# Two output tiles of a fused attention and MLP kernel leave in column halves on two queues

## The chip, the cores and the metric

The kernel runs on one core of a Trainium2 chip. The metric is the device time of one execution in microseconds (us); lower is better. One core has five engines with an instruction stream each: TensorE (PE, matrix products; its weight loads are shown apart as PEld), VectorE (DVE), ScalarE (ACT), GpSimd (POOL) and SyncE (SP, which here only issues transfers and waits). Engines and transfers signal each other by semaphores. A transfer counts its semaphore up in 16 steps, and has landed with the sixteenth.

## The reference

For each of 8 batches and 8 heads (576 positions, 64 features), Nystroem attention with 32 landmarks, and then an MLP with a squared ReLU over all 4608 rows:

```python
A, Bm, C = sm(q, k_lm), sm(q_lm, k_lm), sm(q_lm, k)   # softmax of scaled products
Z = Bm.T / (norm1(Bm) * norminf(Bm) + 1e-6)
for _ in range(6):
    Z = 2 * Z - Z @ Bm @ Z
x = heads_side_by_side(A @ Z @ C @ v)                 # 4608 x 512
out = (maximum(x @ w_in, 0) ** 2) @ w_out             # 512 -> 2048 -> 512, float32
```

`q_lm` and `k_lm` are means over segments of 18 positions.

## The kernel before, in words

The batches are worked through one after the other. For each, the attention part leaves a factor `AT` (with the rows of A) and a product `G` of the rest with `w_in`, so that the first layer of the MLP is `G` times `AT` (`mlp_in`, L821). ScalarE takes the ReLU out of PSUM (L825), VectorE squares it into `gT` (L826). The second layer (`mlp_out`, L834) runs over pairs of batches, whose 1,152 rows are nine tiles of 128 rows, t = 0 to 8: four from the first batch, one (t = 4) of the two tails of 64 rows, four from the second. Each tile is a sum of 16 products (L852) of 128 x 512 in one PSUM bank. ScalarE copies the bank into an SBUF tile `o_sb` (L863), of which there are three in turn, and the tile leaves for the output in HBM (L832 is the line that the profile gives to these transfers, where `leave` calls them).

The order on PE, DVE, ACT and SP is the order in which the program is written down. Strings of tokens, one for each batch (`PLANS`), say when a first-layer tile, a square, an attention step, or some products of the second layer come. `advance(outs, n)` draws n products from the generator `mlp_out`. So within a batch the second layer fills the gaps of the next batch's attention. At the end, after the last batch's plan, the rest of the second layer is run to its end with nothing beside it (the loop over `outs`).

A tile's transfer is not issued at once. It is put on the list `leaving`, and `leave()` issues what is on it, after the third product of the next tile. In the last batch (`b == B - 1`) `leave()` is called straight after the copy. Transfers of the output go by ScalarE's queue (`nc.scalar.dma_start`), with one exception. The very last tile (`final`: b = 7, t = 8) is computed in two parts, 384 columns and then 128. VectorE copies the first part, which leaves by SyncE's queue (`nc.sync`); ScalarE copies the second, which leaves by its own.

SyncE's queue has also carried one load at the start and the transposing transfers (L283, L284, L588) up to batch 7. After the last of these it holds only that 384-column part.

Every transfer that SyncE or ScalarE issues takes the next of eight queue semaphores, DMAHW0 to DMAHW7, in turn, in the order of the program. Before a semaphore is taken again, its last transfer must have landed. GpSimd's transfers have eight of their own, DMASW0 to DMASW7. At the end of the program (L970) SyncE's queue waits for all of them by nine instructions, each with two conditions: first DMASW7 with DMASW6, then DMAHW0 with DMASW5, DMAHW1 with DMASW4, and so on up to DMAHW6 with VectorE's count and DMAHW7 with ScalarE's count. Then come a drain, and two barriers over all engines. In the kernel before, the two parts of the last tile stand on DMAHW4 (SyncE) and DMAHW5 (ScalarE).

Of the kernel before, what the change touches and what calls it, by code (L numbers as in the profile page):

```python
# [17 lines left out]
B = 8  # L18
# [6 lines left out]
DM = 512  # L25
# [61 lines left out]
def kernel(  # L87
# [9 lines left out]
    nc = tc.nc  # L97
# [166 lines left out]
    def ntile(shape, dt=F32, place=0, placed=True):  # L264
        if not placed:
            place = turn[0] = (turn[0] + 1) % 3
        return psum.tile(shape, dt, tag="n%d" % place, bufs=1, name="n%d" % place)
# [560 lines left out]
    leaving = []  # L828

    def leave():  # L830
        while leaving:
            leaving.pop(0)()  # L832

    def mlp_out(b, gT):  # L834

        b0 = b - b % 2
        for t in range(0, NC4) if b % 2 == 0 else range(NC4, 9):
            first, final = (b, t) == (0, 0), (b, t) == (B - 1, 8)
            if final:
                halves = [psum.tile([P, 2, DM], F32, tag="h", bufs=2, name="ops2")[:, 0, 0:w]  # L840
                          for w in (3 * DM // 4, DM // 4)]
            elif (b // 2 + t) % 2:
                halves = [ntile([P, DM], place=2)[:]]
            else:
                halves = [psum.tile([P, DM], F32, tag="o", bufs=1, name="ops")[:]]
            o_sb = mlp.tile([P, DM], F32, tag="o", bufs=3, name="o_sb")
            lo = 0
            for i, ops in enumerate(halves):
                cols = slice(lo, lo + ops.shape[-1])
                lo = cols.stop  # L850
                for f in range(NF):
                    nc.tensor.matmul(ops, lhsT=gT[:, f, t * P:t * P + P],  # L852
                                     rhs=w_out_bf[:, f, cols],
                                     start=(f == 0), stop=(f == NF - 1))
                    if f == 2:
                        leave()
                    if f < NF - 1:
                        yield
                o_h = o_sb[:, cols]
                if final and i == 0:  # L860
                    nc.vector.tensor_copy(o_h, ops)
                else:
                    nc.scalar.copy(o_h, ops)  # L863
                queue = nc.sync if final and i == 0 else nc.scalar
                if t == NC4:
                    for e in range(2):
                        r0 = (b0 + e) * S + NC4 * P
                        leaving.append(partial(queue.dma_start, out[r0:r0 + TAIL, :],
                                               o_h[64 * e:64 * e + TAIL, :]))
                else:  # L870
                    bb, c = (b0, t) if t < NC4 else (b0 + 1, t - NC4 - 1)
                    rows = out[bb * S:bb * S + NC4 * P, :].rearrange("(p c) n -> p c n", c=NC4)
                    leaving.append(partial(queue.dma_start, rows[:, c, cols], o_h))
                if b == B - 1:
                    leave()
                yield
# [28 lines left out]
    def outputs():  # L905
        for b in range(B):
            yield from mlp_out(b, gTs[b // 2])
# [67 lines left out]
```

## Time and profile before

| | us |
|---|---|
| four times | 259.24, 258.86, 258.98, 257.99; median 258.92 |
| the profiled execution | 259.24 |
| its span, from the first to the last instruction | 257.4 |
| PE busy | 248.0 (96% of the span) |
| ACT busy | 154.3 (60%) |
| DVE busy | 173.4 (67%) |
| last part of PE's work ends | 253.8 |

The profile is one execution of the program. Its times count from the start of the span. The page shows each engine's busy share, the chain of work that ended last, the costliest groups of instructions and the transfers. The chain ends with the last computing instruction: what the queues do after that, from 254.1 to 257.4, stands in the rows of the queues alone. A queue's waits and drains are not counted as busy. A wait is recorded with the moment at which it was satisfied and went through, so the time between two such rows is the time waited. The letter q behind an engine (SPq, ACTq) means its instruction queue.

### The profile page before, as it was taken

How to read it: one execution, taken by the hardware profiler on the slowest of the kernel's cores; microseconds unless marked ns; L12 is line 12 of the kernel's file. 1: busy time of each engine (PE TensorE's matmuls, PEld its weight loads, DVE VectorE, ACT ScalarE, POOL GpSimd, SP SyncE). 2: the span in 40 equal slices, each digit the busy share in tenths (PEclk: the TensorE clock that was granted, in tenths of full speed). 3: DMA queues.
4: the chain of work that ended last, by engine and by line, in shares of the span. 5: the costliest groups of instructions: out<-in, count | busy, mean ns of one | idle time of the engine just before them, and what ended most of it. 6: DMA issues, size and time to landing. Idle time of an engine off the chain costs nothing.

```text
span 257.4 us, 6802 instructions
## 1 busy us (share of the span) xinstructions
PE 248.0 (96%) x2784; PEld 147.1 (57%) x2784; DVE 173.4 (67%) x478; ACT 154.3 (60%) x273; POOL 45.4 (18%) x70
## 2 busy tenths in 40 slices
PE   7688899999999999999999999999999999999994
PEld 2555666565645666466646655566646664566442
DVE  5578989658695788658866887677857778334000
ACT  1566798477654785467735765558727774566210
POOL 8934233100301230150000500610000000000000
PEclk9979999999999999999999999999999999999999
DMA  8999999999999999999849799999468113211122
GB/s 187 197 189 203 206 199 197 193 143 159 170 153 165 132 185 179 205 166 211 142 94 144 155 178 222 169 185 179 115 82 167 43 41 94 81 43 42 41 84 83
DMA packets 81216, 37.48 MB, mean 146 GB/s; under 512 B 48800, under 2 KB 75680, under 8 KB 81184
## 3 DMA queue, kind: packets, MB, share of 16 engines
q0 software_dynamic: 39808, 17.83, 56.4%
q1 hardware_dynamic: 36128, 9.97, 25.1%
q10 hardware_dynamic: 5248, 9.24, 11.9%
q8 instruction: 22, 0.36, 0.6%
q14 instruction: 10, 0.08, 0.1%
HBM read 36.70 MB, written 9.44 MB: 179 GB/s over the span
## 4 chain that ended last, share of the span: by engine, by line
PE 91%; DVE 3%; DMA 3%; POOL 1%; issue 1%; ACT 0%; POOLq 0%
PE ops L852 26%; PE h L821 24%; PE n L852 23%; PE g L804 3%; PE n L527 3%; DMA stage<-in_q_dram 3%; PE n L339 2%; PE n L411 2%; PE n L612 1%; PE n L627 1%; PE n L555 1%; PE n L594 1%; PE idle L292 1%; POOL qkt L132 1%; DVE T L660 1%
## 5 line engine op out<-in xcount | busy, mean ns | idle before, releaser
L825 ACT ACTIVATE r<-h 128x576 bf16<-128x576 f32 x128 | 81.1, 653 | 35.7 <-PE h L821 29.2
L852 PE MATMUL ops<-w_out_bf,gT 128*128 128x512 bf16 (+2 forms) x320 | 82.2, 368 | 0.0
L852 PEld LDWEIGHTS <-gT 128*128 128x128 bf16 x592 | 52.4, 97 | 40.6 <-issue 4.6
L852 PE MATMUL n<-w_out_bf,gT 128*128 128x512 bf16 x272 | 72.8, 379 | 0.0
L821 PE MATMUL h<-AT,G 128*128 128x288 bf16 x448 | 70.6, 286 | 0.0
L826 DVE TENSOR_TENSOR gT<-r 128x576 bf16<-128x576 bf16 x128 | 54.8, 447 | 17.5 <-ACT r L825 16.9
L821 PEld LDWEIGHTS <-G 128*128 128x128 bf16 x512 | 48.0, 98 | 24.1 <-DVE AZ L794 0.6
L701 DVE CAST G<-g 128x1024 bf16<-128x1024 f32 x14 | 17.1, 1223 | 7.9 <-PE g L804 7.6
L701 ACT CAST G<-g 128x1024 bf16<-128x1024 f32 x14 | 14.2, 1013 | 11.7 <-PE g L804 11.6
L132 POOL DMA_DIRECT2D raw<-in_k_dram x5 | 4.4, 889 | 80.1 <-DMA AT<-an 35.8
L863 ACT COPY o_sb<-n 128x512 f32<-128x512 f32 x17 | 10.0, 586 | 14.1 <-PE n L852 12.8
L863 ACT COPY o_sb<-ops 128x512 f32<-128x512 f32 (+1 forms) x19 | 10.8, 570 | 10.4 <-PE ops L852 7.3
L527 PEld LDWEIGHTS <-T 128*128 128x128 bf16 x256 | 11.8, 100 | 4.2 <-issue 0.4
L569 DVE TENSOR_REDUCE ra<-EA 128x20 f32<-128x640 f32 (+3 forms) x19 | 13.3, 703 | 1.1 <-ACT EA L532 1.0
L581 DVE TENSOR_TENSOR an<-EA,rra 128x640 bf16<-128x640 f32 (+2 forms) x18 | 13.1, 738 | 0.1
L527 PE MATMUL n<-bd,T 128*128 128x64 bf16 x256 | 13.1, 197 | 0.0
L532 ACT ACTIVATE EC<-n 128x512 bf16<-128x512 f32 x16 | 9.4, 596 | 3.7 <-PE n L527 3.5
L532 ACT ACTIVATE EA<-n 128x512 f32<-128x512 f32 x16 | 9.6, 599 | 3.3 <-PE n L527 1.9
L416 DVE SCALAR_TENSOR_TENSOR EY<-EY,n 128x128 bf16<-128x128 bf16 x25 | 6.9, 277 | 6.3 <-PE n L411 6.2
L292 PE MATMUL idle<-bd 128*128 128x512 bf16 (+1 forms) x27 | 9.1, 462 | 1.5 <-DVE bd L115 1.5
L821 PE MATMUL h<-AZ,G 128*128 128x288 bf16 x64 | 9.9, 286 | 0.3 <-DVE AZ L794 0.3
L339 PEld LDWEIGHTS <-nat 128*128 128x128 bf16 x256 | 8.3, 96 | 3.1 <-issue 0.6
(144 smaller groups left out, 260.5 us busy)
## 6 DMA issues: line engine op xcount, KB each, us to landing
out_dram<-o_sb ACTq DMA_DIRECT2D x31, 256.0 KB, 4.3
vm<-in_v_dram POOLq DMA_DIRECT2D x8, 512.0 KB, 11.5
raw<-in_k_dram POOLq DMA_DIRECT2D x5, 512.0 KB, 7.1
raw<-in_q_dram POOLq DMA_DIRECT2D x5, 512.0 KB, 8.4
w_in_bf<-in_moe_w_in_dram POOLq DMA_DIRECT2D x4, 512.0 KB, 13.3
w_out_bf<-in_moe_w_out_dram POOLq DMA_DIRECT2D x4, 512.0 KB, 17.2
stage<-in_k_dram SPq DMA_DIRECT2D x1, 1024.0 KB, 5.8
stage<-in_k_dram POOLq DMA_DIRECT2D x2, 512.0 KB, 13.8
```

The costliest lines, as they stand in the source:

```text
L292: nc.tensor.matmul(idle[:, 0:width], lhsT=z[:, 0:P], rhs=z[:, 0:width], start=True, stop=True)
L339: nc.tensor.matmul(means[:, ti, p, :], lhsT=src.rearrange("p h d -> p (h d)"), rhs=seg[:, c + (ti if c == NC4 else 0), :], start=(n == 0 a ...
L527: nc.tensor.matmul(sc[:, c, j, :, :], lhsT=X[nm + "T"][:, c, p, :], rhs=BD[:, 1 if nm == "q" else 0, p, 0:64], start=True, stop=True)
L532: nc.scalar.activation(dst, sc.rearrange("p c j i m -> p c (j i m)"), AF.Exp, scale=SCALE)
L569: nc.vector.reduce_sum(ra[:, quads, lo:hi, :], EA[:, quads, lo:hi, :].rearrange("p q c (h m) -> p q c h m", m=M), axis=AX.X)
L581: on.tensor_tensor(an[:, i, lo:hi, :].rearrange("p c (h m) -> p c h m", m=M), EA[:, i, lo:hi, :].rearrange("p c (h m) -> p c h m", m=M), r ...
L701: (act, dve)[n % 2](G[:, :, n * 512:n * 512 + 512], gg[:])
L821: nc.tensor.matmul(h[:, j, 0:HALF], lhsT=G[:, qd, f * P:(f + 1) * P], rhs=AT[:, qd, a0 + j * HALF:a0 + (j + 1) * HALF], start=(qd == 0), s ...
L825: nc.scalar.activation(r.rearrange("p (j t) -> p j t", j=2), h[:, :, 0:HALF], AF.Relu)
L826: return lambda: nc.vector.tensor_tensor(gT[:, f, o:o + S], r[:], r[:], ALU.mult)
L852: nc.tensor.matmul(ops, lhsT=gT[:, f, t * P:t * P + P], rhs=w_out_bf[:, f, cols], start=(f == 0), stop=(f == NF - 1))
L863: nc.scalar.copy(o_h, ops)
```

## The change

In the last batch the tiles t = 6 and t = 7, the last two whole ones, leave in two halves of 256 columns. The first half goes by the queue that took the whole tile before (ScalarE's), the second by SyncE's. Products, copies and the last tile's two parts stay.

```diff
                     rows = out[bb * S:bb * S + NC4 * P, :].rearrange("(p c) n -> p c n", c=NC4)
-                    leaving.append(partial(queue.dma_start, rows[:, c, cols], o_h))
+                    if b == B - 1 and t in (6, 7):
+                        for side, by in ((slice(0, DM // 2), queue), (slice(DM // 2, DM), nc.sync)):
+                            leaving.append(partial(by.dma_start, rows[:, c, side], o_h[:, side]))
+                    else:
+                        leaving.append(partial(queue.dma_start, rows[:, c, cols], o_h))
                 if b == B - 1:
                     leave()
```

There are two transfers more, both on SyncE's queue, which gets four instructions more: two issues, and ahead of each a wait for its queue semaphore (DMAHW3 and DMAHW5; the issue itself waits for ScalarE's copy). The semaphores of all transfers after them shift: t = 6 takes DMAHW2 and 3, t = 7 takes DMAHW4 and 5, and the two parts of the last tile take DMAHW6 (SyncE) and DMAHW7 (ScalarE). The streams of PE, DVE, ACT and POOL keep their instructions and their order.

## Prediction

> **What bounds the kernel now.** I read the page's chain of waits first, then the chain's last pieces, then the timeline of the last 10 us, and last what the queues do after the last computing instruction.
>
> The page's chain that ended last, and the chain's last pieces in order of time (start, length, what):
>
> ```profile
> PE 91%; DVE 3%; DMA 3%; POOL 1%; issue 1%; ACT 0%; POOLq 0%
> ...
> 246.83 6.96 PE ops L852 x48
> 253.79 0.02 issue
> 253.82 0.27 ACT o_sb L863
> ```
>
> TensorE sets the pace to the end. Its last matmul ends at 253.79, ACT copies the last 128 columns out of PSUM, and at 254.08 computing is over. The span is 257.4, so 3.3 us of it lie behind the last arithmetic. The change touches only output transfers; it can win only there, or lose by coming into that stretch.
>
> The timeline of these microseconds (start, length, engine, line, tile), and the page's row on the output transfers (count, size, us from issue to landing):
>
> ```profile
> 246.87 0.59 ACT L863 COPY o_sb<-n 128x512 f32<-128x512 f32 x1 [2.87 <-PE n L852]
> 247.49 0.34 ACTq L832 DMA_DIRECT2D out_dram<-o_sb  x1
> 250.32 0.59 ACT L863 COPY o_sb<-ops 128x512 f32<-128x512 f32 x1 [2.87 <-PE ops L852]
> 250.94 0.34 ACTq L832 DMA_DIRECT2D out_dram<-o_sb  x1
> 252.98 0.56 DVE L861 COPY o_sb<-ops 128x384 f32<-128x384 f32 x1 [13.60 <-PE ops L852]
> 253.56 0.35 SPq L832 DMA_DIRECT2D out_dram<-o_sb  x1
> ...
> 254.11 0.34 ACTq L832 DMA_DIRECT2D out_dram<-o_sb  x1
> ```
> ```profile
> out_dram<-o_sb ACTq DMA_DIRECT2D x31, 256.0 KB, 4.3
> ```
>
> The rows at 247.49 and 250.94 are t = 6 and t = 7, the two that the change splits; 253.56 and 254.11 are the two pieces of t = 8. The last one decides: it lands 1.8 us after its issue. In the trace's records the sixteenth count of its semaphore is at 255.932; that of SP's piece is at 255.715.
>
> Then SP's queue waits for the queue semaphores at L970, one instruction each, in a fixed order: DMAHW0, 1, ... 7. I asked for line 970 on SP's queue in narrow windows (count, ns min/median/max, first and last start):
>
> ```profile
> L970 SPq EVENT_SEMAPHORE  x5: 28/28/28, 254.0 to 254.2; - x5
> L970 SPq EVENT_SEMAPHORE  x1: 28/28/28, 255.7 to 255.7; - x1
> L970 SPq EVENT_SEMAPHORE  x1: 28/28/28, 255.9 to 255.9; - x1
> L970 SPq EVENT_SEMAPHORE  x1: 28/28/28, 256.0 to 256.0; - x1
> L970 SPq EVENT_SEMAPHORE  x1: 28/28/28, 256.5 to 256.5; - x1
> L970 SPq DRAIN  x1: 27/27/27, 256.6 to 256.6; - x1
> ```
>
> The five are one pair of GpSimd semaphores and DMAHW0 to 3, long satisfied. 255.7 is DMAHW4, SP's piece; 255.9 is DMAHW5, ACT's last piece, released 17 ns after its sixteenth count (255.949). DMAHW6 and DMAHW7 are still to come, though their last transfers landed at 238.71 and 242.84. The first costs 70 ns (256.019). The second starts at 256.504, 485 ns later, with nothing to wait for: the other condition it holds, the count of ACT's last copy, was met at 254.09. From 255.949 to 256.504 the program does nothing but walk over two satisfied waits: 0.555 us. From the drain at 256.594 to the end are 0.8 us of barriers that the change doesn't touch.
>
> **The change part by part.** Two transfers more, each taking the next of the eight semaphores in turn, move the last two from DMAHW4 and 5 to DMAHW6 and 7. So the instruction that waits for the last landing is the last of the list.
>
> ACT: the issues at 247.49 and 250.94 stay, with 256 columns in place of 512. The rows price an issue by neither size nor width: 0.338 for 128x512 and for 128x128. Difference 0; ACT then sits idle until 253.82 anyway, 2.5 us of cover.
>
> SP: two issues more and two waits before them. Nearest row 0.348 for its 128x384; 2 x 0.348 + 2 x 0.03 = 0.76 us. They lie at 247.5 and 250.9, on a queue that has nothing else to do, as its waits say (total, times, longest):
>
> ```profile
> SPq L832 <- DVE o_sb L861: 28.3, 1, 28.3
> SPq L970 <- DMA out_dram<-o_sb: 1.6, 2, 1.4
> ```
>
> The 28.3 us before 253.56 are the cover. Behind the new waits in SP's queue stands only its own piece of t = 8: the second half of t = 7 can leave when ACT's copy ends at 250.91, is issued by 251.3, and SP's piece is wanted at 253.56. The cover is 2.3 us. The semaphores that the new issues must find free (DMAHW3, 5, 6) had landed long before.
>
> The halves themselves: pieces of 1,024 bytes a row instead of 2,048. 64 KB landed in 1.8 us, 192 KB in 2.2, 256 KB in 2.4, so 128 KB lies between 1.8 and 2.4. The second half of t = 7 has landed by 250.95 + 2.4 = 253.35, while the data of SP's piece of t = 8 start to move at 254.41. Cost 0, 1.1 us of cover.
>
> A rule that speaks against this: the Trainium skill, "DMA: Bandwidth & Descriptors", section Bandwidth, wants transfers batched towards 1 MiB, since smaller ones are dominated by fixed costs. The rows agree that halving a transfer doesn't halve its time. By the rule the two added fixed costs, some 2 us each by that page, would count if they stood in a row ahead of the end; the trace has them side by side on two queues, so the sum would be the same.
>
> The end: DMAHW6 is then SP's piece (255.715) and DMAHW7 ACT's (255.932), released at 255.949. The drain follows 0.090 later as now, at 256.04 instead of 256.594. Gain 0.555, if the 485 ns do not come back elsewhere.
>
> That is the unknown: no view says why that instruction came late. Of all SP instructions whose conditions I could date, it alone started more than 70 ns after both its conditions and its predecessor. Bounds: if the delay belongs to the place in SP's stream (the 80th traced instruction), the four added instructions push that place onto the wait for DMAHW3, around 254.3, and it is over before 255.7: all 0.555 are won. If it belongs to the moment, some 2.5 us after SP's last issue, or to what stands ahead of the drain, it falls on the drain and only two ordinary waits go: neighbours are 61 to 95 ns apart, 2 x 0.065 = 0.13. Below that nothing is lost, since no instruction is added behind the last landing. I take 0.555, because what the trace measures between 255.949 and 256.504 is the stretch that goes, and a delay anywhere ahead of 255.9 is hidden by the landing.
>
> The Trainium skill, "Runtime: NRT & Kernel Launch", section Instruction fetch mechanics, says that an engine streams its instructions in blocks and that crossing a block is mostly hidden. By that rule the place in the stream would not explain 485 ns, and the sum would be nearer to the 0.13.
>
> Sum against the profiled execution: span 257.4 - 0.555 = 256.85, time 259.24 - 0.555 = 258.69. That time is the highest of the four shown; their median is 258.92, so I put the forecast at 258.92 - 0.555 = **258.4**, 0.21% less.
>
> **The rivals.** (1) The delay comes back on the drain: 258.92 - 0.13 = 258.8. For it: the cause is not shown, and it can't be excluded that the profiled execution alone had it. Against it: nothing ties it to the drain.
> (2) It ends slower: SP's piece of t = 8, until now alone on its queue, runs behind two halves and lands late. Over the whole run an output transfer takes 4.3 us at the median, where the last ones take 1.8 to 2.4. At 4.3 SP's piece would land at 257.86 instead of 255.72, 1.93 after ACT's; less the 0.555 that is +1.4, 260.3. It decides from a landing of 2.15 + 0.22 + 0.56 = 2.9 us on, and passes the bound below from 3.7. Against it: both halves have landed over 1 us before that piece's data move, and loads and transposes that crowd the 4.3 have ended.
> (3) The change doesn't do what it says, since the last transfer isn't on the last semaphore: the built program shows SP's piece on DMAHW6 and ACT's on DMAHW7, so its chance is put at 0; it would give 258.9.
>
> **How the numbers follow.** A measurement of this kernel can tell about 0.3%, 0.78 us, from no change, and the four times before spread over 1.25 us. Forecast 0.55, rival (1) 0.33, rival (2) 0.12. Both likelier cases lie within 0.3%; with the spread of medians some four tenths of the forecast's chance and a tenth of rival (1)'s pass the bound, 0.22 + 0.03 = 0.25 faster; slower 0.12; same 0.63. The range takes both likelier cases with half the spread of the four times, 0.6, below the forecast and 0.5 above rival (1): 257.8 to 259.3.
>
> **What would show it.** In the profile after: nine waits on SP at L970 of which the last starts within 20 ns of the last landing, near 255.95, and the drain 0.09 later; SP's two issues near 247.5 and 250.9; SP's piece still issued at 253.56 and landed in 2.2 us; from the last landing to the span's end 0.9 us instead of 1.5. A gap of 0.4 us between the last wait and the drain is rival (1); a landing of SP's piece over 2.9 us is rival (2). Wrong would be also a gain of more than 0.8 us: nothing here pays for that.

## The result, and the profile after

The changed kernel takes 257.76 us (median of 45 executions) against 258.83 us before (median of 71). The medians are of all executions, while the ratios leave out those that ran some per cent longer as a whole, as did the profiled ones of the first "eight more" and of the third of the change, from which only the stretch behind the last copy is read. The ratio is 0.997, with a 95% interval of 0.9957 to 0.9984: 0.8 us less, between 0.4 and 1.1. The forecast was 0.55 us less, 258.4, in a range of 257.8 to 259.3. Applied to the median of the four times from which the forecast started (258.92), the ratio gives 258.1, inside the range; the median of 257.76 itself lies just under its lower end, beside a median before that is lower too. The profiled execution has a span of 256.3, before 257.4.

That difference of 1.1 us between two single spans isn't the gain. The chain's last pieces after the change (start, length, what):

```profile
246.19 6.96 PE ops L852 x48
253.16 0.02 issue
253.18 0.27 ACT o_sb L863
```

ScalarE's last copy starts 0.64 us earlier than before (253.18 against 253.82), and the last 6.96 us of TensorE are the same. The 0.64 arose before anything that the change touches: from 30 us on, every product of TensorE starts 0.64 us earlier than its counterpart before (a later experiment asks for it again). What is left, from the start of that copy to the end of the span, is 3.12 us against 3.62: 0.49 us. This stretch is the measure in all that follows, since the first 30 us, with their loads, differ by some tenths from execution to execution.

SyncE's issues of the output (count, ns min/median/max, first and last start) and the waits between them, and then the transfers from 230 us on (count, KB, us to landing):

```profile
L832 SPq DMA_DIRECT2D out_dram<-o_sb x3: 332/333/353, 246.8 to 252.9; - x3
L832 SPq EVENT_SEMAPHORE  x2: 17/17/17, 247.2 to 250.7; - x2
```
```profile
out_dram<-o_sb SPq DMA_DIRECT2D x2, 128.0 KB, 2.2
out_dram<-o_sb SPq DMA_DIRECT2D x1, 192.0 KB, 2.2
out_dram<-o_sb ACTq DMA_DIRECT2D x1, 64.0 KB, 1.9
```

SyncE issues three pieces instead of one, in 0.33 to 0.35 us each, at 246.8, 250.3 and 252.9, and the third starts as soon as VectorE's copy allows. Its queue at the end, asked in the same narrow windows as before (the line is now L974):

```profile
L974 SPq EVENT_SEMAPHORE  x4: 28/28/28, 253.3 to 253.5; - x4
L974 SPq EVENT_SEMAPHORE  x1: 28/28/28, 254.0 to 254.0; - x1
L974 SPq EVENT_SEMAPHORE  x2: 28/28/28, 254.1 to 254.2; - x2
L974 SPq EVENT_SEMAPHORE  x1: 28/28/28, 255.2 to 255.2; - x1
L974 SPq EVENT_SEMAPHORE  x1: 28/28/28, 255.4 to 255.4; - x1
L974 SPq DRAIN  x1: 13/13/13, 255.5 to 255.5; - x1
```

The first four end with DMAHW2. Then there is a hole: the wait for DMAHW3, satisfied since 249.14, starts at 254.012, 0.44 us after the instruction ahead of it. DMAHW4 and 5 follow at once. At 255.2 DMAHW6 is released by SyncE's piece, at 255.392 DMAHW7 by ScalarE's, 17 ns after its sixteenth count at 255.375, and the drain comes at 255.459. From the last count to the drain are 0.084 us; before they were 0.662. So the delay that stood behind the last landing (0.46 us) is still there (0.44 us), but now it stands ahead of it, in the time in which SyncE waits anyway.

### The profile page after: what moved, and what is told of

Same layout as the page of the kernel before. It is cut to its first block, busy times and chain, and to the rows that moved or that the text cites. A ratio compares the mean times of both kernels' runs of the same rounds, so it can differ in the third digit from the quotient of the medians.

```text
span 256.3 us, 6806 instructions
## 1 busy us (share of the span) xinstructions
PE 248.0 (97%) x2784; PEld 146.9 (57%) x2784; DVE 172.6 (67%) x478; ACT 154.2 (60%) x273; POOL 45.8 (18%) x70
## 4 chain that ended last, share of the span: by engine, by line
PE 87%; DMA 6%; POOL 4%; DVE 1%; issue 0%; ACT 0%; POOLq 0%
PE ops L852 26%; PE h L821 24%; PE n L852 23%; DMA stage<-in_q_dram 6%; PE g L804 3%; PE n L527 3%; PE n L339 2%; PE n L411 2%; POOL qkt L132 1%; PE n L612 1%; POOL stage L132 1%; PE n L627 1%; POOL w_in_bf L132 1%; PE n L555 1%; POOL seg L203 1%; PE n L310 0%
## 5 line engine op out<-in xcount | busy, mean ns | idle before, releaser
L292 PE MATMUL idle<-bd 128*128 128x512 bf16 (+1 forms) x27 | 9.7, 493 | 1.5 <-DVE bd L115 1.5
```

## The experiments

The theory under test, called that of the place: the instruction at a fixed place in SyncE's stream, the 80th that the profile shows, starts some 0.45 us late, whatever it is. Its rival: what is late is the walk onto the last pair of semaphores. All kernels are edits of the changed one, but for the two rows of "before".

The results in one table, in us from the traces' records. "How late" is from the end of the instruction ahead to the start of the 80th. "Count" is the sixteenth count of the last landing, "copy" the start of ScalarE's last copy.

| kernel | last transfer on | the 80th instruction | how late | count to first drain | copy to count | copy to end |
|---|---|---|---|---|---|---|
| before | DMAHW5 | wait for DMAHW7 | 0.46 | 0.66 | 2.12 | 3.62 |
| before, again | DMAHW5 | wait for DMAHW7 | 0.46 | 0.66 | 2.11 | 3.61 |
| the change | DMAHW7 | wait for DMAHW3 | 0.44 | 0.08 | 2.20 | 3.12 |
| the change, again | DMAHW7 | wait for DMAHW3 | 0.44 | 0.09 | 2.28 | 3.20 |
| the change, third | DMAHW7 | wait for DMAHW3 | 0.46 | 0.09 | 2.28 | 3.19 |
| only t = 7 split | DMAHW6 | wait for DMAHW5 | covered | 0.15 | 2.22 | 3.20 |
| halves on ScalarE | DMAHW7 | wait for DMAHW7 | 0.44 | 0.37 | 2.11 | 3.35 |
| eight more | DMAHW5 | wait ahead of t = 8's issue | 0.46 | 0.20 | 2.21 | 3.23 |
| eight more, again | DMAHW5 | wait ahead of t = 8's issue | 0.45 | 0.20 | 2.21 | 3.25 |
| all on ScalarE | DMAHW7 | second drain | 0.44 | 0.10 | 1.91 | 3.35 |
| t = 5 and 6 split | DMAHW7 | wait for DMAHW3 | 0.46 | 0.09 | 2.21 | 3.11 |
| t = 4's pieces on SyncE | DMAHW7 | wait for DMAHW4 | 0.46 | 0.09 | 2.31 | 3.25 |
| place far ahead | DMAHW7 | wait ahead of t = 8's issue | 0.45 | 0.08 | 2.20 | 3.13 |
| one half on SyncE | DMAHW7 | wait for DMAHW7 | 0.44 | 0.37 | 1.91 | 3.16 |

In the two kernels that give t = 8 wholly to ScalarE the copy itself starts later, behind one issue more, so their last two columns stand apart; for them I count from the start of TensorE's last matmul ("all on ScalarE": 2.36 to the count, 3.79 to the end; "one half on SyncE": 2.36 and 3.60).

### Only one tile split

```diff
-                    if b == B - 1 and t in (6, 7):
+                    if b == B - 1 and t == 7:
```

> Only t = 7 is split. SyncE's stream grows by 2 instructions instead of 4, and the last transfer stands on DMAHW6 of 0 to 7, so one satisfied wait (DMAHW7) is still walked over behind it. Theory of the place (the 80th traced instruction of SyncE's stream starts some 0.45 us late, whatever it is): that place is now the wait for DMAHW5, which stands waiting for the landing of SyncE's own piece anyway; the delay is hidden, and from the sixteenth count of the last landing to the drain it is about 0.16 us (0.66 before, 0.08 after the change); time 0.5 us under before. Theory of the semaphore (the walk onto the last pair, DMAHW7 with ScalarE's count, is late unless it is the pair that ends last): the delay stays behind the last landing, 0.6 us to the drain, time as before within 0.1 us.

The ratio to before is 0.9989 (0.9965 to 1.0012). The end of SyncE's queue:

```profile
L974 SPq EVENT_SEMAPHORE  x6: 28/28/28, 253.6 to 254.0; - x6
L974 SPq EVENT_SEMAPHORE  x1: 28/28/28, 255.5 to 255.5; - x1
L974 SPq EVENT_SEMAPHORE  x1: 28/28/28, 255.8 to 255.8; - x1
...
L974 SPq DRAIN  x1: 7/7/7, 255.9 to 255.9; - x1
```

Two instructions more are enough to bring the late place to the wait at 255.5 (DMAHW5), which is released 16 ns after SyncE's piece has landed, so nothing is to be seen of the delay. The walk over DMAHW7 behind the last landing costs 64 ns, not 485: from the count to the drain 0.154, as the theory of the place had it (0.16; the rival 0.6). The last pair isn't slow in itself.

### The semaphores of the change, SyncE's stream as long as before

```diff
-                        for side, by in ((slice(0, DM // 2), queue), (slice(DM // 2, DM), nc.sync)):
+                        for side, by in ((slice(0, DM // 2), queue), (slice(DM // 2, DM), queue)):
```

> Both tiles are split, but both halves leave by ScalarE's queue: the semaphores are those of the change (last transfer on DMAHW7), SyncE's stream is as long as before the change. Theory of the place: the late instruction is the wait for DMAHW7 itself. It can begin only when the wait before it has been released by SyncE's piece, 0.22 us ahead of the last landing, so some 0.25 us of its 0.45 are left behind the last landing: 0.35 us from the last count to the drain (0.66 before, 0.08 after the change), time 0.3 us under before and 0.25 above the change. Theory of the semaphore: the last pair is the one that ends last, so nothing is left: 0.08 us to the drain, time 0.55 us under before.

The ratio is 0.9982 (0.9951 to 1.0013). The end of SyncE's queue:

```profile
L974 SPq EVENT_SEMAPHORE  x1: 28/28/28, 254.7 to 254.7; - x1
L974 SPq EVENT_SEMAPHORE  x1: 28/28/28, 255.2 to 255.2; - x1
L974 SPq DRAIN  x1: 47/47/47, 255.2 to 255.2; - x1
```

DMAHW6 is released at 254.682. DMAHW7 had its sixteenth count at 254.872, but the wait for it starts at 255.154, 0.444 behind its predecessor. To the drain are 0.37 us (0.35 by the place, 0.08 by the rival). So having the last transfer on the last semaphore is not the whole of it: with the place left where it was, half of what the drain could win is lost.

### The semaphores of before, SyncE's stream longer

```diff
-                        for side, by in ((slice(0, DM // 2), queue), (slice(DM // 2, DM), nc.sync)):
+                        for side, by in ((slice(0, 128), queue), *((slice(o, o + 96), nc.sync) for o in range(128, DM, 96))):
```

> Both tiles leave in five pieces, 128 columns by ScalarE's queue and four of 96 by SyncE's. That is eight transfers more, once round the eight semaphores: the two last pieces stand on DMAHW4 and DMAHW5 as before the change, with DMAHW6 and DMAHW7 to walk over, but SyncE's stream is 10 instructions longer. Theory of the place: the 80th traced instruction lies ahead of the last issue and is hidden; behind the last landing stand two ordinary waits, 0.22 us from the last count to the drain; time 0.4 us under before. Theory of the semaphore: the walk onto DMAHW7 is late as before, 0.66 us to the drain, time as before within 0.1 us.

The ratio is 0.999 (0.9959 to 1.0021). It was profiled a second time:

> The kernel with eight transfers more on SyncE's queue once again, for a second profile. Theory of the place: 0.20 us from the last count to the first drain. In the first profile the instruction transfer was over before the last output transfers moved, and the last count came 2.21 us after the last copy's start. Theory that only an instruction transfer beside the last output transfers puts it back: 2.11. Rival, that other plain transfers on SyncE's queue put it back: 2.2 again.

The second profile, at SyncE's issues (the wait at 252.1 starts 0.446 behind the end of the issue at 251.2) and at the end of its queue:

```profile
L832 SPq DMA_DIRECT2D out_dram<-o_sb x1: 433/433/433, 251.2 to 251.2; - x1
L832 SPq EVENT_SEMAPHORE  x1: 17/17/17, 252.1 to 252.1; - x1
L832 SPq DMA_DIRECT2D out_dram<-o_sb x1: 332/332/332, 252.5 to 252.5; - x1
...
L974 SPq EVENT_SEMAPHORE  x2: 28/28/28, 255.0 to 255.1; - x2
L974 SPq EVENT_SEMAPHORE  x1: 28/28/28, 255.1 to 255.1; - x1
L974 SPq DRAIN  x1: 13/13/13, 255.2 to 255.2; - x1
```

The 80th instruction is now among the issues, and it is late there. At the end the two waits of 255.0 to 255.1 are DMAHW5, the last landing, and DMAHW6, the one after them is DMAHW7. So DMAHW6 and DMAHW7 are still walked over, at 60 ns each: 0.202 us to the drain in both profiles, where the rival wanted 0.66. So the late place explains the larger part of what the drain wins (0.46 of 0.58), and the order of the semaphores the rest (0.12, two ordinary waits).

### All on ScalarE's queue

The edit of the second experiment, and

```diff
-                queue = nc.sync if final and i == 0 else nc.scalar
+                queue = nc.scalar
```

> All pieces, the 384 columns of the last tile too, leave by ScalarE's queue: the semaphores are those of the change (last transfer on DMAHW7), but SyncE's stream is 2 instructions shorter than before the change. Theory of the place: the 80th traced instruction is now the second drain, behind everything; the last count is followed by the release and the first drain in 0.08 us, and then 0.5 us pass to the second drain instead of 0.08. ScalarE issues one transfer more ahead of its last copy, which may put the last landing 0.1 us back. Time as before within 0.2 us. Theory of the semaphore: no delay anywhere, time 0.45 to 0.55 us under before.

The ratio is 0.9981 (0.9951 to 1.0012). The end of SyncE's queue:

```profile
L974 SPq EVENT_SEMAPHORE  x1: 28/28/28, 254.6 to 254.6; - x1
L974 SPq DRAIN  x1: 7/7/7, 254.7 to 254.7; - x1
L974 SPq DRAIN  x1: 129/129/129, 255.2 to 255.2; - x1
```

The last wait and the first drain follow the last landing closely (0.10 us), and then the second drain is 0.443 late. It has no queue semaphore to wait for. So a drain is late in that place as well as a wait. The time to the end behind the last count, 1.43 us, is nearly that of before (1.50), and from the start of TensorE's last matmul to the end pass 3.79 us, before 3.86 to 3.87, after the change 3.38 to 3.46. The place decides.

### How much of the two spans' difference is the change

> The kernel before, unchanged, timed against itself and profiled a second time. It asks what of the 1.1 us between the spans of the two first profiles (257.4 and 256.3) belongs to the change. Theory of the place: the end repeats, 0.66 us from the last count to the first drain and 1.5 us to the span's end, with the 80th traced instruction of SyncE's stream 0.45 us late; the moment at which ScalarE's last copy starts (253.82 before, 253.18 after the change) varies by some 0.5 us from execution to execution, with the loads of the first 30 us. Rival: the change also brings TensorE's end forward, then the last copy starts near 253.8 again. Ratio 1.000, with an interval of about 0.3% either way.

> The changed kernel, unchanged, timed again and profiled a second time. Theory of the place: 0.08 us from the last count to the first drain, 0.93 us to the span's end, the late instruction again the wait for DMAHW3 ahead of the last landing; the last copy starts anywhere from 252.7 to 254. Ratio 0.998, 0.5 us. Rival (the change also brings TensorE's end forward): last copy near 253.2 again, ratio 0.996, 1.1 us.

The ratio of before to itself is 1.001 (0.9984 to 1.0035), that of the change 0.9986 (0.9959 to 1.0013). The last pieces of the chain, first before again, then the change again:

```profile
253.49 0.02 issue
253.51 0.27 ACT o_sb L863
```
```profile
253.53 0.02 issue
253.55 0.27 ACT o_sb L863
```

The last copy now starts at the same time in both, within 0.04 us, and the spans are 257.1 and 256.8. So TensorE's end isn't brought forward; the rival falls. The delays are where they were (table). What was not expected is the column "copy to count": the last landing came 0.08 to 0.17 us later behind the copy in the changed kernel than before.

### What puts the last landing back

Three guesses were tried, and each run was to tell two of them apart.

```diff
-                    if b == B - 1 and t in (6, 7):
+                    if b == B - 1 and t in (5, 6):
```

> The same change made one tile earlier: t = 5 and t = 6 leave in halves, t = 7 whole by ScalarE's queue. Semaphores, length of SyncE's stream and the place of its 80th traced instruction are those of the change. It asks why the last count comes later after the last copy's start in kernels whose SyncE queue has just carried halves (2.20 and 2.28 us after the change, 2.12 and 2.11 before). Theory that SyncE's late halves cost it: the last half by SyncE is 3.5 us earlier, the last count comes 2.11 us after the last copy's start, and from that start to the span's end 3.04 us pass (3.62 and 3.61 before, 3.12 and 3.20 after the change); time 0.55 us under before. Rival, that any plain transfer ahead on SyncE's queue costs it, or chance: 2.20 and 3.13.

Ratio 0.9981 (0.9957 to 1.0006). The count came 2.21 us after the copy: late halves on SyncE's queue aren't the cause.

The next gives both halves to ScalarE, as in the second experiment, and

```diff
-                        leaving.append(partial(queue.dma_start, out[r0:r0 + TAIL, :],
+                        leaving.append(partial((nc.sync if b == B - 1 else queue).dma_start, out[r0:r0 + TAIL, :],
```

> Both halves of t = 6 and t = 7 leave by ScalarE's queue, as in the run with halves on ScalarE's queue, and the two tail pieces of t = 4 in the last batch go by SyncE's queue instead of ScalarE's. The last transfer stands on DMAHW7, SyncE's stream is 3 instructions longer than before the change. Theory of the place: the 80th traced instruction is the wait for DMAHW4, ahead of the last landing, 0.08 us from the last count to the first drain, 0.93 us to the span's end. Theory that SyncE's late halves cost the last landing: last count 2.11 us after the last copy's start, 3.04 us from that start to the span's end, 0.1 us better than the change; time 0.55 us under before. Rival (any plain transfer ahead on SyncE's queue, or chance): 2.20 and 3.13.

> The changed kernel a third time, beside the two above on the same chip. Theory of the place: 0.08 us from the last count to the first drain, 0.93 us to the span's end, the wait for DMAHW3 late by 0.45 us. Theory that SyncE's late halves cost the last landing: last count 2.2 to 2.3 us after the last copy's start; rival, chance: 2.1 to 2.3. Ratio 0.998.

Ratios 0.998 (0.9948 to 1.0011) and 0.9977 (0.9954 to 1.0). The count came 2.31 and 2.28 us after the copy. The first of the two has no half on SyncE's queue and is the latest of all, so that guess is out for good; left were any plain transfers on SyncE's queue ahead, or the 8,192 bytes of instructions that the trace shows on queue q14 0.62 to 0.84 us after the late instruction, where nothing covers it:

```profile
q14 instruction: 1, 0.01, 6.0%
```

That is the row of the change between 254.3 and 255.3, where the last pieces move; before, the same transfer comes at 257.1, when all output has landed. The next kernel moves it to 249.7:

```diff
-                    if b == B - 1 and t in (6, 7):
-                        for side, by in ((slice(0, DM // 2), queue), (slice(DM // 2, DM), nc.sync)):
+                    if b == B - 1 and t in (5, 6, 7):
+                        cuts = (0, 192, 352, 512) if t == 7 else (0, 128, 224, 320, 416, 512)
+                        for k, lo_hi in enumerate(zip(cuts, cuts[1:])):
+                            by, side = nc.sync if t < 7 and k else queue, slice(*lo_hi)
+                            leaving.append(partial(by.dma_start, rows[:, c, side], o_h[:, side]))
```

> Ten transfers more: t = 5 and t = 6 in five pieces each (128 columns by ScalarE's queue, four of 96 by SyncE's), t = 7 in three by ScalarE's queue. The last transfer stands on DMAHW7, and the 80th traced instruction of SyncE's stream is the wait ahead of its issue for t = 8, which comes up some 4 us ahead of that issue. The instruction transfer that follows the late instruction by 0.6 to 1.0 us in every profile so far then runs near 250, well ahead of the last output transfers. Theory of the place: 0.08 us from the last count to the first drain, 0.93 us to the span's end. Theory that this instruction transfer, when it runs beside the last output transfers, puts the last count back: last count 2.11 us after the last copy's start, 3.04 us from that start to the span's end, 0.1 us better than the change. Rival, that other plain transfers on SyncE's queue put it back, however early: 2.2 to 2.3 us and 3.13 to 3.25. Time 0.5 us under before.

Ratio 0.9997 (0.9965 to 1.003). To the drain 0.08 us, as the place has it, but the count still came 2.20 us after the copy. In the two profiles of "eight more" that transfer is over 0.77 and 0.85 us after the start of TensorE's last matmul, when the data of t = 8 begin to move (0.84), and there too the count came at 2.21 us. So the instruction transfer beside the last output isn't the cause either, or not of the first 0.1 us.

The last kernel takes the other plain transfers and the late place apart:

```diff
-                queue = nc.sync if final and i == 0 else nc.scalar
+                queue = nc.scalar
...
-                        for side, by in ((slice(0, DM // 2), queue), (slice(DM // 2, DM), nc.sync)):
+                        for side, by in ((slice(0, DM // 2), queue), (slice(DM // 2, DM), nc.sync if t == 7 else queue)):
```

> As the run with everything on ScalarE's queue, except that SyncE's queue carries the second half of t = 7. Its stream is then as long as before the change, the late instruction is the wait for DMAHW7 (0.35 us from the last count to the first drain by the theory of the place), and nothing of t = 8 is on SyncE's queue. In all profiles so far the last count came later (2.45 to 2.57 us after the start of TensorE's last matmul, against 2.36 to 2.37) in just those kernels that have other plain transfers on SyncE's queue near the end, and these are also the kernels whose late instruction lies ahead of the last landing. Here the two are taken apart. Theory that the plain transfers on SyncE's queue put the last count back: 2.45 or more. Rival, that it goes with the late instruction's place: 2.36.

One time was taken, 257.98 beside 258.23 of before. The kernel to set it beside is "all on ScalarE", from which it differs in that one plain transfer: the count came 2.355 us after the start of TensorE's last matmul, there 2.358. A plain transfer on SyncE's queue isn't enough.

The packets show where the loss sits. These are the rates of all transfers (GB/s) in 40 slices of 0.08 us from the start of ScalarE's last copy, first before, then the change again:

```profile
GB/s 0 0 0 0 0 0 0 134 365 403 403 384 442 269 135 256 333 135 19 0 0 0 0 0 0 0 0 0 0 0 0 0 0 0 0 0 0 0 0 0
```
```profile
GB/s 0 0 0 0 0 0 0 154 422 422 346 442 422 212 116 243 327 154 19 0 102 0 0 0 0 0 0 0 0 0 0 0 0 0 0 0 0 0 0 0
```

In both the output's last packet ends 1.51 us after the copy's start (the 102 is the instruction transfer), but the sixteenth count comes at 2.11 to 2.12 in the one and at 2.28 in the other. So it is in all twelve profiles in which SyncE carries the 384 columns: the last packet ends 1.76 to 1.77 us after the start of TensorE's last matmul in each, and the count follows 0.60 to 0.61 us later in the three without the loss, 0.69 to 0.81 in the nine with it. The data move as before; what comes later is the count behind them. (With t = 8 wholly on ScalarE's queue the last packet ends at 1.92 to 1.93 and the count follows 0.43 later, so these two kernels are compared with each other only.)

Why it comes later stays open, with two readings. Either the loss goes with the late place being ahead of the landing, by a way that no view shows, or it needs SyncE's own piece of t = 8 behind other plain transfers on its queue. In all nine profiles with the loss both hold, in the other five neither does. SyncE's piece itself lands 2.18 to 2.27 us after its issue in the nine, and 2.15 to 2.18 in the three of the five that have it. A kernel that parts these two wasn't tried.

## Why the prediction was right

**The end of the program bounds what the change can do.** Right: TensorE's last 6.96 us, ScalarE's copies and the start of SyncE's last issue stand against each other as before.

**The satisfied waits and the delay behind the last landing.** Right, and the largest term: the last wait went through 17 ns after the last landing, and SyncE's piece landed 2.2 us after its issue, as the signs named ahead had it. The forecast was that 0.555 us go between the last landing's release and the drain. The traces give 0.662 - 0.084 = 0.578 from count to drain.

**The unknown delay belongs to the place in SyncE's stream.** Taken for the likelier, with the bound that four added instructions would push it in front of the landing, onto the wait for DMAHW3. It stood there, 0.44 to 0.46 us late, in all three profiles of the change, and in every other kernel the same ordinal was late wherever it fell. (With one tile split a longer wait covers it; there the instruction transfer on q14 comes 1.09 us after the end of the 79th instruction, in the others 1.08 to 1.30.) That the choice came out was in part luck: no row of the profile before spoke for the place against the drain. Rival (1), that it would fall on the drain, is out for the change; of the kernel that shortens SyncE's stream it is true, for the second drain. The moment, some 2.5 us after SyncE's last issue, is out too: the late instruction starts 2.94 us after the start of that issue before, 1.08 after the change, and 5.26 with one half on SyncE.

The Trainium skill, "Runtime: NRT & Kernel Launch", section Instruction fetch mechanics, was weighed against the place: crossing a block of instructions is mostly hidden. The traces show 0.44 to 0.46 us in the open at one fixed place, with an instruction transfer behind it every time, so at this place the delay was not hidden, and the 0.13 to which the prediction saw that rule lead didn't come. That the place is a block's edge would fit and is not shown: no run tried what the place itself depends on.

**Issues on both queues are free.** Right: 0.33 to 0.35 us each on SyncE, 0.36 for ScalarE's two halves where a whole tile took 0.34, nothing waits for them.

**The halves don't disturb the last pieces: cost 0.** This is the term that was mis-sized. The last count comes 0.08 to 0.18 us later after the copy's start than before (2.20 to 2.28 against 2.11 to 2.12). It isn't rival (2), which wanted SyncE's piece to land 4.3 us after its issue: it took 2.2, and the data of both pieces moved as before. What the sum left out is that the count behind the data can come later. So the net from the copy to the end is 3.61 to 3.62 before and 3.12 to 3.20 after, 0.40 to 0.49 us, where 0.555 was forecast. The halves' own landing was put at 1.8 to 2.4 us: SyncE's took 2.1 to 2.4, ScalarE's, beside them, 2.4 to 2.6. Both halves of t = 7 had still landed over 1 us before the data of t = 8 moved. The fixed cost of some 2 us that the prediction takes from a page of the Trainium skill is given there for transfers that GpSimd issues; these go by SyncE's and ScalarE's queues, where the rows above hold.

**The time.** 0.8 us by the ratio, with 0.4 to 1.1 around it, holds the 0.555 and nearly all of the 0.40 to 0.49 of the traces. Its middle lies at the 0.8 that was named as a sign of being wrong. What it has beyond 0.5 no trace shows as belonging to the change, and in the two later sessions the ratio was 0.9986 and 0.9977, 0.4 and 0.6 us. I take the rest for the scatter of the early loads, which is not shown. So the mechanism is shown by the ends of the traces, and that the time came out as near as it did is not further evidence for it. Whether the kernels of the experiments differ in time can't be told: all their intervals overlap and reach 1.000. The verdicts on them rest on the traces' ends alone.

None of the variants beats the change by what the traces can tell. The nearest, with t = 5 and 6 split, has 3.11 us from the copy to the end, 0.01 under the lowest of the change's own three (3.12 to 3.20).

## What to carry to other kernels

Look behind the last arithmetic: the profile's chain ends there, but the queues' rows go on, and a wait that starts long after its condition was met is time in which no view shows any work. To find out whether such a delay sits in an instruction or in its place, change the number of instructions ahead of it on that queue and see which one is late next. And compare single profiles of a change this small by a stretch that starts at a common event, here the last copy, not by their spans.

## What the runs showed of the hardware that was not expected

One place in SyncE's stream, the 80th traced instruction, started 0.44 to 0.46 us late in every profile in which no longer wait covered it (13 of 14), whether it was a wait at the end, a wait ahead of an issue or a drain. An instruction transfer of 8,192 bytes on q14 started 0.62 to 0.84 us after it in these.

The second and later of several plain issues in a row on one queue take longer than the first: SyncE's four of 96 columns took 0.33 to 0.35 and then 0.42 to 0.46 us each, ScalarE's second half 0.45 where the first took 0.34.

In the last microseconds, with little else in flight, 64, 128, 192 and 256 KB landed in 1.6 to 2.0, 1.9 to 2.6, 2.1 to 2.3 and 2.3 to 2.5 us after their issue. Two halves issued on two queues at once took 2.1 to 2.6 us each, hardly less than the whole tile (2.3 to 2.5); of two halves on one queue the first took 1.9.

Of such a landing a good part lies behind the data: from the end of the last packet to the sixteenth count passed 0.60 to 0.81 us with t = 8 on two queues, and 0.43 with both its pieces on one.
